# Head of a fused attention and gated-MLP kernel: another order for the V projections of the first chunk, and one load moved to SyncE's queue

## The chip, the cores and the metric

The kernel runs on one core of a Trainium2 chip. The metric is device time in microseconds (us) of one execution, the median over several runs.

The engines are named as in the profile: PE is TensorE's matmul, PEld its weight load, DVE is VectorE, ACT is ScalarE, POOL is GpSimd and SP is SyncE. SP does no arithmetic here: it issues DMA transfers. ACT can issue them too. Each engine works through its own instructions in order.

## The reference, cut to what matters

The input `x` has 2048 rows of 640 numbers in bf16. Its rows are normalised, and the result goes into two branches that are added to `x`.

```
def _A_ref(x, wqkv, wo):
    B, S, D = x.shape
    H = 32; Dh = D // H; W = 256
    qkv = (lambda x, *d: x.transpose(*d))((x @ wqkv).reshape(B, S, 3, H, Dh), 2, 0, 3, 1, 4)
    q, k, v = qkv[0], qkv[1], qkv[2]
    scores = jnp.einsum("bhqd,bhkd->bhqk", q, k) * (Dh ** -0.5)
    idx = jnp.arange(S)
    mask = (idx[:, None] - idx[None, :] >= 0) & (idx[:, None] - idx[None, :] < W)
    scores = jnp.where(mask[None, None], scores, -1e9)
    p = _softmax(scores, axis=-1)
    o = jnp.einsum("bhqk,bhkd->bhqd", p, v)
    return (lambda x, *d: x.transpose(*d))(o, 0, 2, 1, 3).reshape(B, S, D) @ wo

def _B_ref(x, w_gate, w_up, w_down):
    g = jnp.einsum("bsd,df->bsf", x, w_gate)
    u = jnp.einsum("bsd,df->bsf", x, w_up)
    h = _sigmoid(g) * u
    return jnp.einsum("bsf,fd->bsd", h, w_down)

x = A_x
xn = _layernorm(x, axis=-1)
return x + _A_ref(xn, A_wqkv, A_wo) + _B_ref(xn, B_w_gate, B_w_up, B_w_down)
```

The change touches the layer norm of the first 512 rows and their V columns, `xn @ wqkv[:, 1280:1920]`.

## The kernel before

**Chunks and blocks.** The 2048 rows are worked through in four chunks of 512 rows, and each chunk has four blocks of 128 rows, numbered 0 to 3. A block lies in SBUF with its 128 rows on the partitions. The later chunks' projections, the MLP matmuls and the attention steps are mixed by a small planner (`Fill`, L533) that hands out matmul work by cost between attention steps. The first chunk has nothing to be mixed with: its head is written out by hand at L614 to L648, one call after another, and the order of the calls is the order of the instructions on each engine (`tc.manual_schedule()`).

**What the head does for each block s of chunk 0.**

1. `load_rows(s, queue)` (L171) loads 128 x 640 numbers of `x` (160 KB).
2. Mean and deviation come in one of two ways. Blocks 0 and 2 use DVE: `ln_half` (L245) takes the statistics of one half of the columns, `ln_mv` (L251) joins the two halves, and `root` (L587) takes the square root on ACT. Blocks 1 and 3 use ACT: `mean_act` (L596) sums the row, `root_act` (L602) sums the squares and takes the root.
3. `norm` (L592) or `norm_act` (L608) takes the reciprocal and scales the rows, both on DVE.
4. `transpose_rows` (L272) turns the block on PE, five matmuls of 128 x 128 into a PSUM tile `pt`, and the function given as `copy` brings it into `xnT[0]`, on DVE or ACT. For block 0 this is done in two pieces.
5. `project_v(0, s, hf)` (L319) multiplies the block with one half of V's columns, `hf` 0 or 1, 320 each: a group of five matmuls into a PSUM tile. `copy_v` (L327) brings it to SBUF in bf16, on DVE or ACT, into `vt`. `proj_v` is the two together.

The group of block s and half hf is called "s, hf" or just the two digits, so 01 is block 0, second half. There are eight of them, and their PSUM tiles rotate through four buffers of `ps_d` (two warm-up tiles have used that pool before).

**The loads.** `load_v(hf)` (L174) loads one half of V's columns (400 KB), `load_wqkv(0)` and `load_wqkv(1)` the Q and the K columns (800 KB each), and `load_gu(0)` (L195) the first halves of the MLP's gate and up weights (960 KB each). All of these are issued by SP, one after the other, as are the rows of blocks 0, 1 and 3. The rows of block 2 are issued by ACT (L235), behind a first activation that loads ACT's table. Two `clear` transfers end the list; what SP issues next are the projected Q columns.

**After the head.** `g_qk(0)` (L360) projects Q and K of chunk 0, ten groups of five matmuls at L295. Each group's result is copied (DVE for Q, ACT for K), written to a scratch tensor in DRAM and read back, spread over the partitions as the scores need it (L311). Then `load_rest` (L203) issues the second halves of the MLP's weights, and the planner's mixture begins: gate and up matmuls (L401, L408), score steps (L472) with exponentials on ACT (L477) and masks on POOL (L480), the products with V (L504), and the output projections (L422, L429).

While ten matmuls on zeros (L236 to L239) run at the start, no rows have landed yet.

The head as it stands, with the eight groups:

```
transpose 0, 00, transpose 1, 01, 10, transpose 2, 11, 20, transpose 3, 21, 30, 31
```

Of the kernel before, what the change touches and what calls it, by code (L numbers as in the profile page):

```python
# [107 lines left out]
def kernel(  # L108
# [11 lines left out]
    nc = tc.nc  # L120
# [44 lines left out]
    def load_wqkv(part):  # L165
        nc.sync.dma_start(out=wqkv[:, :, part * D:(part + 1) * D],
                          in_=wqkv_r[:, :, part * D:(part + 1) * D])
# [3 lines left out]
    def load_rows(s, queue):  # L171
        queue.dma_start(out=xc[0][:, s, :], in_=xr[:, s, :])

    def load_v(hf):  # L174
        a = 2 * D + hf * HALF
        nc.sync.dma_start(out=wqkv[:, :, a:a + HALF], in_=wqkv_r[:, :, a:a + HALF])
# [2 lines left out]
    load_rows(1, nc.sync)  # L179
    load_v(0)  # L180
    load_rows(3, nc.sync)
    load_v(1)
    load_wqkv(0)
    load_wqkv(1)
# [47 lines left out]
    nc.gpsimd.memset(eps, EPS)  # L232
    scr = const.tile([P, 1], FP32, name="scr")
    nc.scalar.activation(out=scr, in_=eps, func=SQRT)
    load_rows(2, nc.scalar)  # L235
    for n in (6, 4):  # L236
        ps = ps_d.tile([P, CW], FP32, name="pwarm", tag="d")
        for k in range(n):
# [6 lines left out]
    def ln_half(c, s, a, stats=None):  # L245
        if a == 0:
            stats = lnp.tile([P, 2, nc.vector.BN_STATS_DIM], FP32, name="stats")
        nc.vector.bn_stats(out=stats[:, a, :], in_=xc[c][:, s, a * HALF:(a + 1) * HALF])  # L248
        return stats

    def ln_mv(stats, mv=None):  # L251
        if mv is None:
            mv = lnp.tile([P, nc.vector.BN_AGGR_DIM], FP32, name="mv")
        nc.vector.bn_aggr(out=mv, in_=stats)
        return mv

    def ln_block(c, s, mv=None):
        return ln_mv(ln_half(c, s, 1, ln_half(c, s, 0)), mv)
# [13 lines left out]
    def transpose_rows(s, copy, lo=0, hi=DC):  # L272
        pt = ps_h.tile([P, DC, P], BF16, name="pt")
        for d in range(lo, hi):
            nc.tensor.transpose(pt[:, d, :], xns[0, s][:, d * P:(d + 1) * P], ident)  # L275
        copy(out=xnT[0][:, lo:hi, s * P:(s + 1) * P], in_=pt[:, lo:hi, :])  # L276
# [42 lines left out]
    def project_v(c, s, hf):  # L319
        ps = ps_d.tile([P, CW], FP32, name="pv", tag="d")  # L320
        for d in range(DC):
            nc.tensor.matmul(ps[:, 0:HALF], lhsT=xnT[c][:, d, s * P:(s + 1) * P],  # L322
                             rhs=wqkv[:, d, 2 * D + hf * HALF:2 * D + (hf + 1) * HALF],
                             start=(d == 0), stop=(d == DC - 1))
        return ps

    def copy_v(c, s, hf, ps, copy):  # L327
        v3 = vt[c * SBC + s][:, 0:H * VW].rearrange("p (h d) -> p h d", d=VW)
        copy(out=v3[:, hf * 16:(hf + 1) * 16, 0:DH],  # L329
             in_=ps[:, 0:HALF].rearrange("p (h d) -> p h d", d=DH))  # L330

    def proj_v(c, s, hf, copy=nc.vector.tensor_copy):
        copy_v(c, s, hf, project_v(c, s, hf), copy)
# [253 lines left out]
    def root(mv):  # L587
        r = lnp.tile([P, 1], FP32, name="rstd")
        nc.scalar.activation(out=r, in_=mv[:, 1:2], func=SQRT, bias=eps)
        return r  # L590

    def norm(s, mv, r):  # L592
        nc.vector.reciprocal(r, r)
        norm_block(0, s, mv, r)

    def mean_act(s):  # L596
        xn = lnp.tile([P, D], BF16, name="xn")
        neg = lnp.tile([P, 1], FP32, name="neg")
        nc.scalar.activation(out=xn, in_=xc[0][:, s, :], func=IDENTITY, scale=-1.0 / D, accum_out=neg)
        return xn, neg  # L600

    def root_act(s, xn, neg):  # L602
        r = lnp.tile([P, 1], FP32, name="rstd")
        nc.scalar.activation(out=xn, in_=xc[0][:, s, :], func=SQUARE, bias=neg, accum_out=r)
        nc.scalar.activation(out=r, in_=r, func=SQRT, bias=eps, scale=1.0 / D)
        return r

    def norm_act(s, xn, neg, r):  # L608
        nc.vector.reciprocal(r, r)
        nc.vector.tensor_scalar(out=xn, in0=xc[0][:, s, :], scalar1=neg[:, 0:1],  # L610
                                scalar2=r[:, 0:1], op0=ADD, op1=MULT)
        xns[0, s] = xn
# [4 lines left out]
    act, dve = nc.scalar.copy, nc.vector.tensor_copy  # L617
# [7 lines left out]
    v00 = project_v(0, 0, 0)  # L625
    norm_act(1, xn1, neg1, r1)
    xn3, neg3 = mean_act(3)
    transpose_rows(1, act)
    mv2 = ln_block(0, 2)
    r2 = root(mv2)  # L630
    v01 = project_v(0, 0, 1)
    copy_v(0, 0, 0, v00, dve)
    norm(2, mv2, r2)
    r3 = root_act(3, xn3, neg3)
    v10 = project_v(0, 1, 0)
    copy_v(0, 0, 1, v01, dve)
    transpose_rows(2, dve)
    v11 = project_v(0, 1, 1)
    norm_act(3, xn3, neg3, r3)
    copy_v(0, 1, 0, v10, act)  # L640
    copy_v(0, 1, 1, v11, act)
    v20 = project_v(0, 2, 0)
    transpose_rows(3, dve)
    copy_v(0, 2, 0, v20, act)
    proj_v(0, 2, 1, dve)
    proj_v(0, 3, 0, act)
    proj_v(0, 3, 1, dve)
    nc.scalar.activation(out=scr, in_=neghalf[:, 0:1], func=EXP)  # L648
    banks.close()
    ps_s = banks.enter_context(tc.tile_pool(name="ps_s", bufs=1, space=bass.MemoryType.PSUM))  # L650
# [134 lines left out]
```

## Time and profile before

| what | value |
|---|---|
| runs | 314.15, 314.97, 314.70, 315.43 us; median 314.83 |
| the profiled execution | 314.15 us, its span 312.4 us |
| PE busy | 304.7 us, 98% of the span |
| PEld / DVE / ACT / POOL busy | 56% / 51% / 62% / 50% |
| granted TensorE clock in the record | 1.00 |
| moved by DMA | 35.71 MB, mean 114 GB/s |

The span runs from the first to the last instruction of the profiled execution; 1.75 us of its time lie around the span. A timeline line gives start, length, engine, line, operation, output and input, count, and in brackets how long the engine was idle before and what released it. Lengths of matmuls that follow each other overlap, since the array is pipelined: the step from one to the next is shorter than the length of one. The same holds to a smaller degree on DVE and ACT.

How the DMA engines stand in the head can be seen in the windows of 3 us: their busy share is 1.00 to 1.06 from 3 to 18 us and the rate 286 to 396 GB/s, so that transfers queue behind each other there; it falls to 0.43 between 27 and 30 us and is back at 1.00 or more from 33 us.

### The profile page before, as it was taken

What the parts mean: (1) busy time and instruction counts of PE and PEld (TensorE: products, weight loads), DVE (VectorE), ACT (ScalarE), POOL (GpSimd) and SP (SyncE); (2) the same over time, 40 slices, a digit from 0 to 9 for tenths busy, and PEclk for the clock granted to TensorE, in tenths of its full rate; (3) what the DMA queues carried; (4) which work ended last, traced back from release to release, by engine and by line L of the source; (5) the groups of instructions that cost most, each with busy time, mean ns of one, the idle gap of its engine ahead of it and who ended that gap; (6) DMA issues with size and microseconds to landing.
All of it is one profiled execution on the core that took longest, in us unless ns stands there. A gap on an engine that the chain in (4) does not pass through costs nothing.

```text
span 312.4 us, 10513 instructions
## 1 busy us (share of the span) xinstructions
PE 304.7 (98%) x4627; PEld 175.5 (56%) x4663; DVE 160.3 (51%) x316; ACT 192.2 (62%) x177; POOL 155.7 (50%) x239
## 2 busy tenths in 40 slices
PE   8999999999999999999999999999999999999995
PEld 3554444556557655644567665744556675544774
DVE  3643746548695264289826154362723536262523
ACT  5614787697764648787673647768585547778000
POOL 3000576576872827567382627546362835555000
PEclk9999999999999999999999999999999999999999
DMA  7995999664663153720025213630000213000002
GB/s 228 375 330 176 308 386 162 228 175 154 198 79 106 44 157 100 233 82 2 2 44 86 87 57 97 215 119 2 2 3 2 72 58 109 0 4 0 4 21 65
DMA packets 37614, 35.71 MB, mean 114 GB/s; under 512 B 10272, under 2 KB 37024, under 8 KB 37536
## 3 DMA queue, kind: packets, MB, share of 16 engines
q1 hardware_dynamic: 37136, 34.76, 38.3%
q8 instruction: 36, 0.59, 0.8%
q10 hardware_dynamic: 432, 0.28, 0.3%
q14 instruction: 10, 0.08, 0.1%
HBM read 23.63 MB, written 10.26 MB: 108 GB/s over the span
## 4 chain that ended last, share of the span: by engine, by line
PE 95%; DMA 2%; DVE 1%; issue 1%; DVEq 0%
PE y L422 17%; PE pu L408 17%; PE pg L401 17%; PE pqk L295 14%; PE ps L472 9%; PE y L429 7%; PE acc L504 7%; PE pv L322 7%; DMA xc<-in_A_x_dram 2%; DVE stats L248 0%; PE pt L275 0%; DVE h L412 0%; DVE xn L268 0%; DVE v L329 0%; DVE xn L433 0%
## 5 line engine op out<-in xcount | busy, mean ns | idle before, releaser
L480 POOL TENSOR_SCALAR_AFFINE_SELECT pT<-pT 128x512 bf16<-128x512 bf16 (+2 forms) x192 | 147.2, 798 | 129.1 <-ACT pT L477 129.0
L477 ACT ACTIVATE pT<-ps 128x2048 bf16<-128x2048 f32 x76 | 142.7, 1878 | 63.7 <-PE ps L472 59.0
L412 DVE SCALAR_TENSOR_TENSOR h<-th,pu 128x512 bf16<-128x512 f32 x48 | 32.7, 682 | 60.8 <-PE pu L408 49.6
L408 PE MATMUL pu<-xnT,wu 128*128 128x512 bf16 x228 | 59.2, 380 | 0.7
L401 PE MATMUL pg<-xnT,wg 128*128 128x512 bf16 x225 | 57.8, 380 | 1.0 <-issue 0.5
L422 PE MATMUL y<-wd,h 128*128 128x320 bf16 (+2 forms) x396 | 57.0, 296 | 0.0
L295 PE MATMUL pqk<-xnT,wqkv 128*128 128x512 bf16 x191 | 45.5, 381 | 0.5
L422 PEld LDWEIGHTS <-h 128*128 128x128 bf16 x396 | 36.5, 98 | 14.3
L404 ACT ACTIVATE th<-pg 128x512 f32<-128x512 f32 x48 | 28.6, 596 | 14.5 <-PE pg L401 13.9
L401 PEld LDWEIGHTS <-wg 128*128 128x128 bf16 x240 | 22.3, 98 | 25.3 <-issue 0.2
L408 PEld LDWEIGHTS <-wu 128*128 128x128 bf16 x240 | 21.9, 98 | 25.4 <-issue 0.6
L472 PEld LDWEIGHTS <-kT 20*64 20x64 bf16 x1856 | 20.6, 103 | 24.2 <-issue 22.3
L295 PEld LDWEIGHTS <-wqkv 128*128 128x128 bf16 x200 | 22.6, 119 | 18.0 <-issue 0.6
L472 PE MATMUL ps<-qT,kT 20*64 20x128 bf16 (+4 forms) x1856 | 32.5, 239 | 0.0
L433 DVE SCALAR_TENSOR_TENSOR rows<-y,rows 128x320 bf16<-128x320 f32 x30 | 14.5, 489 | 33.2 <-PE y L429 33.0
L514 DVE STREAM_TRANSPOSE t<-acc 128x512 f32<-128x512 f32 x32 | 22.0, 710 | 18.1 <-PE acc L504 17.8
L526 DVE TENSOR_TENSOR on<-t,rec 128x320 bf16<-128x320 f32 (+4 forms) x48 | 27.5, 574 | 1.1
L322 PE MATMUL pv<-wqkv,xnT 128*128 128x320 bf16 x160 | 24.1, 302 | 0.3 <-DVE xnT L276 0.2
L429 PE MATMUL y<-wo,oc 128*128 128x320 bf16 (+2 forms) x165 | 24.2, 295 | 0.0
L504 PE MATMUL acc<-pT,v 128*32 128x64 bf16 (+3 forms) x1376 | 23.2, 223 | 0.1
L504 PEld LDWEIGHTS <-v 128*32 128x32 bf16 x1376 | 18.6, 97 | 7.9 <-ACT pT L477 1.7
L322 PEld LDWEIGHTS <-xnT 128*128 128x128 bf16 x160 | 14.9, 98 | 7.3 <-DVE xnT L276 1.0
(46 smaller groups left out, 134.3 us busy)
## 6 DMA issues: line engine op xcount, KB each, us to landing
qT<-sq SPq DMA_DIRECT2D x7, 512.0 KB, 5.5
sq<-st SPq DMA_DIRECT2D x20, 128.0 KB, 4.0
sk<-st SPq DMA_DIRECT2D x20, 128.0 KB, 2.8
rows<-in_A_x_dram SPq DMA_DIRECT2D x15, 160.0 KB, 2.2
out_dram<-rows SPq DMA_DIRECT2D x15, 160.0 KB, 1.8
kT<-sk SPq DMA_DIRECT2D x4, 512.0 KB, 5.7
wg<-in_B_w_gate_dram SPq DMA_DIRECT2D x2, 960.0 KB
wu<-in_B_w_up_dram SPq DMA_DIRECT2D x2, 960.0 KB, 9.9
```

Source lines behind the costliest of these rows:

```text
L295: nc.tensor.matmul(ps, lhsT=wt[:, m, :], rhs=xnT[c][:, d, :], start=(d == 0), stop=(d == DC - 1))
L322: nc.tensor.matmul(ps[:, 0:HALF], lhsT=xnT[c][:, d, s * P:(s + 1) * P], rhs=wqkv[:, d, 2 * D + hf * HALF:2 * D + (hf + 1) * HALF], start=( ...
L401: nc.tensor.matmul(pg, lhsT=part(wg, d, f), rhs=xnT[c][:, d, :], start=(d == 0), stop=(d == DC - 1))
L404: nc.scalar.activation(out=th, in_=pg, func=TANH, scale=0.5)
L408: nc.tensor.matmul(pu, lhsT=part(wu, d, f), rhs=xnT[c][:, d, :], start=(d == 0), stop=(d == DC - 1))
L412: nc.vector.scalar_tensor_tensor(out=h, in0=th, scalar=1.0, in1=pu, op0=ADD, op1=MULT)
L422: nc.tensor.matmul(y[:, 0:cut[1] - cut[0]], lhsT=ht[c, f][:, s * P:(s + 1) * P], rhs=wd[:, f, cut[0]:cut[1]], start=(f == 0), stop=False)
L429: nc.tensor.matmul(y[:, 0:cut[1] - cut[0]], lhsT=oc[c, m][:, s * P:(s + 1) * P], rhs=wo[:, m, cut[0]:cut[1]], start=False, stop=(m == DC - 1))
L472: nc.tensor.matmul(ps[hf * U:(hf + 1) * U, i, col * U:(col + n) * U], lhsT=qk["k", kc, g // GH][32 * i:32 * i + DH, g % GH, key:key + U], ...
L477: nc.scalar.activation(out=pt[:, :, 0:CW], in_=ps, func=EXP, scale=SCALE)
L480: nc.gpsimd.affine_select(out=out, in_=in_, pattern=[[0, HG], [0, n], [sign, width]], compare_op=GE, fill=0.0, base=base, channel_multipli ...
L504: nc.tensor.matmul(acc[32 * i:32 * i + 32, q * U:(q + n) * U], lhsT=v[:, h * VW:h * VW + 32], rhs=pt[:, i, col * U:(col + n) * U], start=( ...
```

## The change

The rows of block 2 are issued by SP, between those of block 3 and V's second half, and no longer by ACT. Then the hand-written order of the head is another one:

- TensorE's order becomes transpose 0, 00, transpose 1, 10, 01, transpose 3, 11, transpose 2, 30, 31, 20, 21. The number of matmuls is the same.
- The copy of transpose 1 goes from ACT to DVE, and stands on DVE between the two halves of block 2's statistics.
- ACT's square sum and root for block 3 come ahead of the root for block 2, and DVE scales block 3 ahead of block 2.
- The copies of 00 and 01 go from DVE to ACT. ACT now copies 00, 10, 01, 11, 30 and 20; DVE copies 31 and 21.

DMA transfers signal their landing through eight counters that are used in turn, and a transfer waits until the one that used its counter before has landed. With block 2's rows at another place in the list, the transfers of the head wait for other ones than before.

```
@@ -179,6 +179,7 @@
     load_rows(1, nc.sync)
     load_v(0)
     load_rows(3, nc.sync)
+    load_rows(2, nc.sync)
     load_v(1)
     load_wqkv(0)
     load_wqkv(1)
@@ -232,7 +233,6 @@
     nc.gpsimd.memset(eps, EPS)
     scr = const.tile([P, 1], FP32, name="scr")
     nc.scalar.activation(out=scr, in_=eps, func=SQRT)
-    load_rows(2, nc.scalar)
     for n in (6, 4):
         ps = ps_d.tile([P, CW], FP32, name="pwarm", tag="d")
         for k in range(n):
@@ -625,26 +625,26 @@
     v00 = project_v(0, 0, 0)
     norm_act(1, xn1, neg1, r1)
     xn3, neg3 = mean_act(3)
-    transpose_rows(1, act)
-    mv2 = ln_block(0, 2)
+    r3 = root_act(3, xn3, neg3)
+    half2 = ln_half(0, 2, 0)
+    transpose_rows(1, dve)
+    mv2 = ln_mv(ln_half(0, 2, 1, half2))
+    v10 = project_v(0, 1, 0)
+    copy_v(0, 0, 0, v00, act)
     r2 = root(mv2)
     v01 = project_v(0, 0, 1)
-    copy_v(0, 0, 0, v00, dve)
+    norm_act(3, xn3, neg3, r3)
     norm(2, mv2, r2)
-    r3 = root_act(3, xn3, neg3)
-    v10 = project_v(0, 1, 0)
-    copy_v(0, 0, 1, v01, dve)
+    copy_v(0, 1, 0, v10, act)
+    transpose_rows(3, dve)
+    v11 = project_v(0, 1, 1)
+    copy_v(0, 0, 1, v01, act)
     transpose_rows(2, dve)
-    v11 = project_v(0, 1, 1)
-    norm_act(3, xn3, neg3, r3)
-    copy_v(0, 1, 0, v10, act)
     copy_v(0, 1, 1, v11, act)
-    v20 = project_v(0, 2, 0)
-    transpose_rows(3, dve)
-    copy_v(0, 2, 0, v20, act)
-    proj_v(0, 2, 1, dve)
     proj_v(0, 3, 0, act)
     proj_v(0, 3, 1, dve)
+    proj_v(0, 2, 0, act)
+    proj_v(0, 2, 1, dve)
     nc.scalar.activation(out=scr, in_=neghalf[:, 0:1], func=EXP)
```

## The prediction

> **What bounds the kernel now.** I read the page's chain of waits first, then the same chain for the first 15 us, then the timelines of TensorE, its weight loads, VectorE and ScalarE there, and last the stretch after 30 us where weights land late. The chain's shares by engine:
>
> ```profile
> PE 95%; DMA 2%; DVE 1%; issue 1%; DVEq 0%
> ```
>
> TensorE sets the end everywhere but in the head. So a change in the head is worth what it takes from the time at which TensorE is through with V and begins the Q/K projections (pqk). The head's part of the chain (start, length, what):
>
> ```profile
> 0.80 2.34 DMA xc<-in_A_x_dram
> 3.17 4.63 DMA xc<-in_A_x_dram
> ...
> 7.82 0.90 DVE stats L248 x2
> ...
> 9.51 0.46 DVE xn L268
> ...
> 10.01 0.45 PE pt L275 x5
> ```
>
> The second load is row block 2, issued on ScalarE's queue at 3.17 and landed at 7.80. Its statistics, root and scaling follow, and TensorE gets block 2's transpose only at 10.01. TensorE and its weight loads in that time:
>
> ```profile
> 5.50 0.74 PE L275 MATMUL pt<-ident,xn 128*128 128x128 bf16 x5
> 6.47 1.12 PE L322 MATMUL pv<-wqkv,xnT 128*128 128x320 bf16 x5 [0.24 <-DVE xnT L276]
> 7.43 0.44 PE L275 MATMUL pt<-ident,xn 128*128 128x128 bf16 x5
> 7.92 1.59 PE L322 MATMUL pv<-wqkv,xnT 128*128 128x320 bf16 x10
> 10.01 0.45 PE L275 MATMUL pt<-ident,xn 128*128 128x128 bf16 x5 [0.50 <-DVE xn L268]
> ...
> 12.02 2.28 PE L322 MATMUL pv<-wqkv,xnT 128*128 128x320 bf16 x15
> 14.13 0.38 PE L295 MATMUL pqk<-xnT,wqkv 128*128 128x512 bf16 x1
> ```
>
> Call T1 the transposes of block 1 and "10" the V group of block 1, first half. Fifteen matmuls stand between 12.02 and 14.13, less one wait of 0.07: 2.04/15 = 0.136 us each, 0.68 for a group. A transpose set holds TensorE 0.28 (10.01 to the next group at 10.30 on the full timeline; 11.74 to 12.02). From T1's last issue at 7.71 (7.43 + 0.28) to pqk at 14.13 are 6.42 us; seven groups and two sets are 7 x 0.68 + 2 x 0.28 = 5.32. TensorE waits 1.10 in it: 0.21 for group 01 (7.71 to 7.92), 0.68 for T2 (9.33 to 10.01), 0.2 in three small ones.
>
> **The change part by part.** Everything up to T1 is untouched, so T1's results stand at 7.87 (7.43 + 0.44).
>
> *T1's copy goes from ScalarE to VectorE, behind the first half of block 2's statistics.* The rows:
>
> ```profile
> 6.72 0.45 DVE L610 TENSOR_SCALAR xn<-xc,neg,rstd 128x640 bf16<-128x640 bf16 x1
> 7.82 0.89 DVE L248 BATCH_NORM_STATS2 stats<-xc 128x6 f32<-128x320 bf16 x2 [0.65 <-DMA xc<-in_A_x_dram]
> 10.50 0.49 DVE L276 COPY xnT<-pt 128x640 bf16<-128x640 bf16 x1
> ...
> 7.91 0.69 ACT L276 COPY xnT<-pt 128x640 bf16<-128x640 bf16 x1 [1.00 <-PE pt L275]
> ```
>
> VectorE is free at about 7.13 (its next operation starts 0.41 after a 0.45 one). The half statistics take 0.49: 7.13 to 7.62, if block 2 is there. The copy then waits only for T1 and starts at 7.91 as ScalarE's did, but takes 0.49 for 0.69: done at 8.40 for 8.60. A weight load follows a copy by 0.05 (10.99 to 11.04), so group 10 starts at 8.45.
>
> *Block 2's load moves to SyncE's queue.* Its landing there is not in the trace. Lower bound: block 3's rows (same size, issued at 2.19 directly ahead, awaited by ScalarE until 6.08) plus 164 kB at the 357 GB/s of the window from 6 to 9 us, 0.46: 6.5. Upper bound: V's second half, issued at 2.76 and first used at 7.92, took at most 5.16; from the new issue at 2.63 that is 7.8. I take 6.5, the row it is nearest to. The copy of T1 is hit only from a landing after 7.42 (7.91 - 0.49). At 7.8 it would start at 8.21 (statistics step 0.41), 0.30 later.
>
> The Trainium skill (DMA: Bandwidth & Descriptors, "Issuing engines are not separate DMA queues") says that all queues run on the same 16 engines and interleave, and another issuer saves only issue time. That speaks against a gain from the move. By it the load would come only its earlier issue sooner, at about 7.3; the trace's 4.63 us on ScalarE's queue against 3.9 on SyncE's speaks for a little more. By the rule as by the row, the copy of T1 is not delayed.
>
> SyncE issues one more load (0.43, the L176 row's length), so V's second half, the Q and K weights, the gate weights and the clears are issued 0.43 later. V's second half, in use at 7.92 before, is wanted at 9.14 now; the Q weights (issued at 3.24, 6.9 to landing: 10.1) at 13.8. SyncE stands idle from 10.7 to 16.1, where the delay ends. Without that cover group 01 would lose at most 0.43. ScalarE loses the issue (0.44 at 3.17); its next operation, at 3.65, waited for block 1's rows, and that chain has 0.7 to spare (root ready at 5.80, used at 6.53): nothing.
>
> *TensorE's new order: 10, 01, T3, 11, T2, 30, 31, 20, 21.* 10 is now first after T1 with nothing to cover the copy, so TensorE waits 7.71 to 8.45 = 0.74. Is each input there in time after that?
> - 01 at 9.14 needs block 0 and V's second half: there.
> - T3 at 9.82 needs block 3 scaled. VectorE: statistics' second half 8.32 to 8.80, aggregate 0.21, reciprocal 0.15, scaling 0.45, with gaps of 0.04: 9.68. ScalarE's root for it: mean 6.08 to 6.91, square 0.81, read and root to 8.2. Margin 0.14.
> - 11 at 10.10: there. T2 at 10.78 needs block 2 scaled: root 9.07 to 9.36, then reciprocal and scaling after block 3's: 10.3.
> - 30 at 11.06 needs T3's copy: T3's results at 10.3, VectorE free then, 0.49 and 0.05: 10.85.
> - 31, 20, 21 follow; T2's copy is done at 11.8, wanted at 12.42.
>
> So the wait is 0.74 for 1.10. pqk starts at 8.45 + 5.32 = 13.77 against 14.13: **0.36 earlier**.
>
> *Copies of V.* ScalarE gets 00 and 01 (2 x 0.43) and loses T1's (0.69): 0.17 more, under its 3.4 us of idle before 14.1. VectorE gets 0.49 and loses 0.98. The accumulators rotate over four buffers: 30 takes that of 00, freed at 8.6, wanted at 11.06; the others have more room. Without the cover the Exp table load at 14.10 would slip, and its first use is past 31 us. All this costs nothing.
>
> *Does 0.36 last?* The transfers after 24 us are paced by the DMA engines (share 1.00 and above from 33 to 42 us), so landings need not move with TensorE. The tight one is the second half of the up weights:
>
> ```profile
> 30.57 0.53 SPq L197 DMA_DIRECT2D wu<-in_B_w_up_dram  x1
> ...
> DMA to landing us min/median/max: 9.9/9.9/9.9
> ...
> 40.79 0.76 PEld L408 LDWEIGHTS <-wu 128*128 128x128 bf16 x5
> ```
>
> It lands at 40.47 and is used at 40.79: 0.32 of room, less 0.05 from landing to use. If the landing stays, 0.27 of the gain survives; if it moves along, 0.36. I take 0.3. After that, the chain is TensorE to the end.
>
> **The sum.** The profiled execution: 314.15 - 0.3 = 313.85. It is the lowest of four (to 315.43), 0.68 under their median of 314.83, so the forecast for a median is 314.5.
>
> The Trainium skill (TensorE: Matmul & The Clock Gate, Part 1) says that the array runs at half rate until a free-running window of about 3.4 us was busy. From the first warm-up matmul at 1.25 the rise could fall anywhere from 4.7 to 8.1, another place in each run, an estimate from that page. This trace has it inside group 00: T0 took 0.74 and T1 0.44. By an early rise the gain would be near 0.5, by the latest about -0.2, since the old order's wait for T2 hides cold matmuls and the new order has no such wait left. The sum goes by the trace.
>
> **The rivals.**
> - *Hidden anyway*, 314.8. The weights' landing at 40.47 slips by a little, or the transposed rows of the second chunk (by DMA, wanted near 56 us) do, and the 0.3 is gone. For it: 0.32 of room. Against it: those loads start from Q/K spreads that partly follow TensorE.
> - *All of the 1.10 goes*, 313.7. It needs T1's copy to be covered; in the new order nothing stands between T1 and group 10, so only runs that scatter low would show it.
> - *The clock rises later* (slower). Place: the 0.74 hole at 7.71, in the change's kernel alone. A cold group costs about 0.65 more (the ten warm-up matmuls of 512 columns took 4.45, about 0.43 each, where five later ones step in 1.08, 0.22 each; so 320 columns 0.27 for 0.136), T1 0.30 (0.74 - 0.44), the rest of group 00 about 0.4. If the rise waits until 10 and 01 are done: 0.4 + 0.30 + 2 x 0.65 = 2.0 less 0.36, 1.6 slower: 316.5. It decides from a rise after 7.7. Against it: the rise at about 7 lies ahead of the first changed instruction.
> - *The load isn't sooner on SyncE's queue.* At the bound of 7.8 the gain is 0.06: 314.8.
>
> **How the numbers follow.** Within 0.3% (0.94 us, about what a measurement of this kernel can tell from no change; the four runs spread over 1.28): the forecast 0.46, hidden 0.13, load not sooner 0.07: 0.66. Faster 0.18: all of the 1.10 gone 0.12, low scatter 0.06. Slower 0.16: the clock 0.11, high scatter 0.05. Predicted is the likeliest, 314.5. The range: down to the full 1.10, 313.7; up through no gain to the highest run before, 315.5; the clock's 316.5 is left out.
>
> **What would show it.** T1's copy on VectorE at 7.9 for 0.5 us, group 10 at about 8.45, no wait of TensorE over 0.1 from there to pqk, pqk at 13.8; block 2's statistics starting at 7.1 with no wait for the load; the weight load of L408 near 40.5. Wrong: block 2's load awaited past 7.4, T3 waiting for its scaling, cold matmuls (0.27 a step) in groups 10 or 01, or pqk at 13.8 with the end not moved.

## The result, and the profile after

The changed kernel took 313.77 us (median of 34 runs, 313.02 to 316.30); the kernel before took 315.01 us over 56 runs (314.08 to 315.99). The ratio is 0.9967, with a 95% interval of 0.9959 to 0.9975: 1.04 us, or 0.33%, faster (0.0033 x 315.01; by the two medians 1.24). A run more than 1.5% above the fastest of its kernel counts as slow and enters no ratio; that was one run, in call 3. The gain is just past the 0.3% that the prediction had named as its border, and about three times the 0.3 us that it had worked out.

The profiled execution of the changed kernel took 313.39 us with a span of 311.7, against 314.15 and 312.4. The shares by engine of the chain of waits, on the page:

```profile
PE 95%; DMA 1%; DVE 1%; issue 1%; SPq 1%; DVEq 0%
```

TensorE still sets the end, and DMA's share went from 2% to 1%. The head of that chain (start, length, what):

```profile
2.76 4.14 DMA xc<-in_A_x_dram
...
6.92 0.49 DVE stats L248
7.42 0.44 DVE xnT L276
...
7.91 1.53 PE pv L322 x10
```

Block 2's rows land at 6.90 instead of 7.80. But they are still in the chain: the first half of their statistics stands on VectorE ahead of T1's copy, and the copy ends at 7.86. They hold it up by next to nothing, though, since T1's own results stand only at 7.32 (6.87 + 0.45):

```profile
7.36 0.49 DVE L276 COPY xnT<-pt 128x640 bf16<-128x640 bf16 x1
```

From 7.91 TensorE waits no more than 0.07 in all up to the Q/K projections (13.30 - 7.91 = 5.39, where the prediction's sum has 5.32). TensorE's timeline in the same stretch:

```profile
5.33 0.45 PE L275 MATMUL pt<-ident,xn 128*128 128x128 bf16 x5
6.12 0.85 PE L322 MATMUL pv<-wqkv,xnT 128*128 128x320 bf16 x5 [0.34 <-DVE xnT L276]
6.87 0.45 PE L275 MATMUL pt<-ident,xn 128*128 128x128 bf16 x5
7.91 1.53 PE L322 MATMUL pv<-wqkv,xnT 128*128 128x320 bf16 x10 [0.59 <-DVE xnT L276]
...
13.30 2.54 PE L295 MATMUL pqk<-xnT,wqkv 128*128 128x512 bf16 x10
```

Two things are to be seen. Block 0's transposes take 0.45 here and took 0.74 before, so the clock rose earlier in this execution, ahead of anything that TensorE does in another order: the recorded clock goes to full at 4.88, against 7.06 in the first profile. T1 starts at 6.87 for 7.43 by it. And the Q/K projections (pqk) start at 13.30 for 14.13: 0.83 earlier, where the prediction had 0.36. The next line is from the weight loads near 40 us:

```profile
40.28 0.76 PEld L408 LDWEIGHTS <-wu 128*128 128x128 bf16 x5 [0.36 <-DMA wu<-in_B_w_up_dram]
```

The seventh up group started at 40.79 before, without a wait. Now TensorE's weight loads stand 0.36 until the second half of the up weights has landed, and start 0.51 ahead: 0.32 of the 0.83 is gone there. (The chain of this profile names VectorE's scaling, which ended at the same time; call 3 separates the two.) Score matmuls near 203 us that take 0.52 for 0.36 cost another 0.16. What is left when VectorE's last operation starts, before and after:

```profile
309.06 0.29 DVE xn L433
```
```profile
308.71 0.29 DVE xn L433
```

0.35 of the gain is left there, and 0.76 between the two whole executions. So 0.41, more than half, arises behind the last matmul, where little more than the last output transfers is under way. The table further below comes back to this.

### The profile page after: what moved, and what is told of

Same layout as the page of the kernel before. It is cut to its first block, busy times and chain, and to the rows that moved or that the text cites. A ratio compares the mean times of both kernels' runs of the same rounds, so it can differ in the third digit from the quotient of the medians.

```text
span 311.7 us, 10513 instructions
## 1 busy us (share of the span) xinstructions
PE 304.0 (98%) x4627; PEld 175.2 (56%) x4663; DVE 160.0 (51%) x315; ACT 192.1 (62%) x178; POOL 155.7 (50%) x239
## 4 chain that ended last, share of the span: by engine, by line
PE 95%; DMA 1%; DVE 1%; issue 1%; SPq 1%; DVEq 0%
PE y L422 17%; PE pu L408 17%; PE pg L401 16%; PE pqk L295 14%; PE ps L472 9%; PE y L429 7%; PE pv L322 7%; PE acc L504 7%; DMA xc<-in_A_x_dram 1%; DVE h L412 0%; SPq L172 0%; DVE xn L268 0%; PE pt L275 0%; DVE stats L248 0%; DVE xnT L276 0%
```

## The experiments

Twelve more measurements were made in three calls. The kernels of one call shared a chip and its runs of the kernel before, whose median was 315.66, 315.11 and 314.96 us in the three calls; so a kernel is compared with others of its own call.

### Call 1: which part does it, and how steady is the head?

**The kernel before once more**, without an edit.

> The kernel before, unchanged, for a second profile and for the spread of its head. Open is why the change gave about 1.0 us where the prediction's sum has 0.36 at the head and 0.3 at the end. Theory 'clock': the clock's rise moves from run to run, but the Q/K projections start near 14.1 as in the first profile, since the wait for block 2 hides it; the first profile is typical. Theory 'landing': block 2's rows land at another time in each run on ScalarE's queue, mostly later than the first profile's 7.80, and the projections start later than 14.3 here. Times the same as before within 0.1% by both.

Measured: 315.28 us (12 runs), ratio 0.9992 (0.9976 to 1.0008): no difference. Its median is 0.38 below that of the other runs of the same kernel in the call, which shows how little a difference of that size between two medians says. The chain in its profile:

```profile
3.19 4.85 DMA xc<-in_A_x_dram
...
10.26 0.45 PE pt L275 x5
```

Block 2's rows land at 8.04, 0.24 later than in the first profile. T2 starts 0.25 later, and pqk at 14.38, also 0.25 later. In these two profiles the landing moves and takes pqk with it one for one.

**The load alone.**

```
     load_rows(3, nc.sync)
+    load_rows(2, nc.sync)
     load_v(1)
...
-    load_rows(2, nc.scalar)
```

> The old order with block 2's rows on SyncE's queue, between block 3's and V's second half. Theory 'load' (the gain comes from block 2's rows being there sooner): rows at 6.9, statistics from 7.1, block 2 scaled at about 9.5 for 9.95, its transposes at 9.6 for 10.01, Q/K projections at about 13.7; most of the gain, a ratio of 0.997 to 0.998. Theory 'order' (the gain comes from the new order and the faster copy of T1): less than a third of the gain, 0.999 to 1.000, with the projections at 13.9 or later, since V's second half, issued later, now holds back group 01.

Measured: 313.98 us (11 runs), ratio 0.9952 (0.9935 to 0.9969). By the runs the load alone brings the gain here. The head of its profiled execution, 314.57 us, is not what the first theory expected: the loads were late in it (V's first half landed at 6.45, against 5.57 in the first profile; block 2's rows at 7.35), and pqk started at 14.13, no earlier than in the first profile. V's second half, now behind block 2's rows, landed at 8.62 and held back group 01, as the second theory has it. Where the gain of the runs arises is therefore not shown by this profile alone.

**The order alone.**

```
     nc.scalar.activation(out=scr, in_=eps, func=SQRT)
+    load_rows(2, nc.scalar)
...
-    load_rows(2, nc.sync)
```

applied to the changed kernel, so that only the new order is left.

> The new order with block 2's rows left on ScalarE's queue. Theory 'load': the statistics' first half waits for the rows until 7.8 and the copy of T1 stands behind it, so T1's copy starts at 8.2 and group 10 at 8.75, projections at 14.0 to 14.1; ratio 0.999 to 1.000, and slower in executions in which the rows land later than 7.9. Theory 'order': group 10 by 8.5, projections by 13.8, ratio 0.997 to 0.998.

Measured: 315.59 us (12 runs, 314.40 to 318.14), ratio 1.0009 (0.9985 to 1.0034). The order alone brings no gain that shows. The chain:

```profile
3.19 5.54 DMA xc<-in_A_x_dram
...
8.76 0.49 DVE stats L248
9.25 0.40 DVE xnT L276
...
9.70 1.53 PE pv L322 x10
```

The rows land at 8.73, and the copy of T1 waits behind their statistics. Group 10 starts at 9.70 and pqk at 15.02. By the prediction's own sum a landing after 7.86 makes the new order slower than the first profile's 14.13. The profiled execution, 316.53 us, was 0.94 above the median of its runs, and the head is not all of it: near 58 us TensorE waited another 1.05 for the second chunk's transposed rows.

**The changed kernel, with the late weights in pieces.** The second halves of the gate and up weights are loaded in two column pieces each.

```
-    def load_gu(k):
-        for t, w in ((wg, B_w_gate), (wu, B_w_up)):
-            nc.sync.dma_start(out=t[k], in_=w.rearrange("(c p) f -> p c f", p=P)[:, :, k * FS:(k + 1) * FS])
+    def load_gu(k, parts=1):
+        n = FS // parts
+        for lo in range(0, FS, n):
+            for t, w in ((wg, B_w_gate), (wu, B_w_up)):
+                nc.sync.dma_start(out=t[k][:, :, lo:lo + n],
+                                  in_=w.rearrange("(c p) f -> p c f", p=P)[:, :, k * FS + lo:k * FS + lo + n])
...
-            load_gu(k)
+            load_gu(k, 2)
```

> The changed kernel with the second-half gate and up weights loaded in two pieces each (columns 0 to 383 of both, then the rest), so that the first up columns land near 37.5 rather than 40.2. In the profile of the changed kernel TensorE came 0.84 ahead to 39.9 and started the seventh up group at 40.28, 0.51 ahead of the kernel before. Theory 'landing cap': that group then starts as early as TensorE comes, and the end is 0.2 to 0.4 us earlier than the changed kernel, a ratio to the kernel before of 0.9955 to 0.9965. Theory 'no cap' (the wait there was VectorE's scaling, as the chain has it, or a later wait takes the gain anyway): the same as the changed kernel, 0.9967 within 0.0006.

Measured: 313.48 us (6 runs), ratio 0.9943 (0.9922 to 0.9964). The interval is too wide to tell it from the changed kernel, which was not in this call; call 3 puts them side by side. In its profile pqk starts 0.45 ahead of the first profile, and the seventh up group, at 40.33 without a wait, 0.46: nothing is lost near 40 us.

### Call 2: load against order on one chip, and what makes the load late

**The changed kernel** and **the load alone**, both again.

> The changed kernel, unchanged, on the same chip as the next three. Theory 'load' (in the first call the old order with the load on SyncE's queue gave 0.9952, the new order with the old load 1.0009): 0.995 to 0.997, and equal to the load alone within 0.001. Theory 'both' (the new order adds the 0.36 that the prediction worked out): 0.001 faster than the load alone. In its profile: block 2's rows between 6.6 and 7.4, Q/K projections at 13.2 with an early rise of the clock and at 13.5 to 13.8 with one near 7.

> The old order with block 2's rows on SyncE's queue, beside the changed kernel on one chip. Theory 'load': 0.995 to 0.997, equal to the changed kernel within 0.001; Q/K projections at 13.6 to 14.0. Theory 'both': 0.001 slower than the changed kernel.

Measured: 313.92 us (12 runs), ratio 0.9960 (0.9940 to 0.9979), for the changed kernel; 314.41 us (12 runs), 0.9978 (0.9956 to 1.0001), for the load alone. By the medians the order adds 0.49 us to the load, but the intervals overlap, and the second one includes no change; in call 1 the load alone had been 1.68 below the kernel before, here 0.70. So the times leave open what the order adds. The chain of the load alone tells where it would come from:

```profile
3.23 5.91 DMA wqkv<-in_A_wqkv_dram
...
9.18 1.52 PE pv L322 x10
```

In the old order group 01 is next after T1. With block 2's rows moved ahead of it, V's second half lands at 9.14 in this execution and becomes the wait; pqk starts at 14.65. In the changed kernel group 10 comes first, needs only V's first half, and group 01 finds V's second half there. An estimate, from the landings and transposes of the two profiles of the load alone: in the new order their pqk would have started 0.36 and 0.28 earlier.

**The load on ScalarE's queue, but first of all.**

```
     load_rows(1, nc.sync)
+    load_rows(2, nc.scalar)
...
-    load_rows(2, nc.scalar)
```

applied to the kernel before; the load is now ScalarE's first instruction, issued at 0.79.

> The old order with block 2's rows still on ScalarE's queue, but as its first instruction, ahead of the activation table, so issued at about 0.8 rather than 3.17. Theory 'place in the line' (what counts is when the load is issued, not by which engine): rows by 4.5, block 0's and block 1's up to 0.5 later since they share the DMA engines; no wait for block 2 before its transposes beyond that for ScalarE's root, projections at 13.7 to 14.0, ratio 0.996 to 0.999. Theory 'queue' (ScalarE's queue is served behind SyncE's backlog): rows after 7 as before, projections at 14.1 to 15.0, ratio 1.000.

Measured: 314.35 us (12 runs), ratio 0.9983 (0.9962 to 1.0003), pqk at 14.05. Block 2's rows landed at 4.05, between blocks 0 (3.87) and 1 (4.44). Nothing waits for them any more; the chain goes another way:

```profile
2.76 5.54 DMA wqkv<-in_A_wqkv_dram
...
8.34 1.57 PE pv L322 x10
```

V's second half takes the place of the wait again, and blocks 0 and 1 came 0.7 to 0.8 later, where 0.5 was expected. pqk is just past the expected 13.7 to 14.0. ScalarE's queue as such isn't slow.

**The changed kernel with the load one place later**, behind V's second half.

```
-    load_rows(2, nc.sync)
     load_v(1)
+    load_rows(2, nc.sync)
```

> The changed kernel with block 2's rows on SyncE's queue behind V's second half rather than ahead of it. Theory 'load': the rows land at 7.9 to 8.6, the statistics' first half and behind it the copy of T1 wait for them, one for one, so group 10 starts 0.41 + 0.49 + 0.05 after the landing, near 9.1 (8.4 with the rows at 7), and the projections at 14.2 to 14.8; ratio 0.999 to 1.001. Theory 'order': 0.996 to 0.998, projections by 13.8.

Measured: 314.40 us (12 runs), ratio 0.9981 (0.9959 to 1.0003), 0.48 above the changed kernel by median. The chain:

```profile
3.23 4.64 DMA xc<-in_A_x_dram
...
7.89 0.49 DVE stats L248
8.38 0.40 DVE xnT L276
...
8.83 1.53 PE pv L322 x10
```

On SyncE's queue, issued at 3.23, the rows land at 7.86. On ScalarE's queue, issued at 3.17, they had landed at 7.80. So the earlier landing comes not from the queue but from the place: ahead of the 400 KB of V's second half. Group 10 starts 0.97 after the landing, by the 0.41 + 0.49 + 0.05 of the expectation (0.95), and pqk at 14.15, as in the first profile of the kernel before. The median lies 0.71 below the kernel before's all the same, though the ratio's interval reaches 1.0003.

### Call 3: the cap near 40 us, and an attempt to go further

**The changed kernel a third time, and with the weights in pieces.**

> The changed kernel, unchanged, as the mark for the next three on the same chip: 0.995 to 0.997 of the kernel before.

> The changed kernel with the second-half gate and up weights in two pieces each, now beside the changed kernel. Theory 'landing cap' (part of the head's gain is lost near 40 us, where the seventh up group waits for weights that land at 40.2 to 41.1): 0.2 to 0.5 us faster than the changed kernel by median. Theory 'no cap', or the transposed rows of the second chunk, wanted near 56 us, take the gain instead: equal within 0.15 us.

Measured: 314.10 us (12 runs), ratio 0.9975 (0.9962 to 0.9989), and 313.63 us (6 runs), 0.9955 (0.9938 to 0.9973). The pieces are 0.47 faster by median; the intervals overlap. In both profiles pqk starts at 13.39, so the two heads end alike. The changed kernel's TensorE at 31 us and its chain at 41 us read:

```profile
31.24 0.42 PE L472 MATMUL ps<-qT,kT 20*64 20x320 bf16 x16 [0.38 <-DMA kT<-sk]
```
```profile
31.45 9.60 DMA wu<-in_B_w_up_dram
41.04 0.05 issue
41.09 1.25 PE pu L408 x5
```

Of the 0.74 that the head was ahead of the first profile of the kernel before, 0.48 is lost at 31.24 (31.50 there), where K columns are read back late. Then the up weights, issued at 31.45 instead of 30.57, land at 41.04 after another 0.58 of waiting, and TensorE comes out 0.29 behind. With the pieces, the weight loads and the later chain:

```profile
40.05 0.76 PEld L411 LDWEIGHTS <-wu 128*128 128x128 bf16 x5
```
```profile
51.08 4.53 DMA xnT<-xn
55.61 0.04 issue
55.65 2.32 PE pqk L298 x10
```

Here the whole 0.74 passes 40 us, and 0.44 of it passes the next late landing, the second chunk's transposed rows at 55.61 (pqk of that chunk at 55.65, for 56.09 in the first profile). The profiles show the wait for the up weights, which is gone in both profiles with the pieces, and the wait behind it. VectorE's scaling was not the cause: with the pieces it ends at 40.34, and the group starts ahead of that, at 40.05. That the wait for the up weights is worth the 0.47 of the medians is likely, not shown: 6 runs stand against 12, and part of the difference between these two profiles arose at 31 us.

**All rows ahead of V.** The row loads of blocks 3 and 2 go ahead of V's first half, block 2's statistics ahead of block 0's copy, group 00 behind T1, group 01 behind transpose 3, and ScalarE's root for block 2 ahead of its copy of 00; the second kernel has the weights in pieces too.

```
     load_rows(1, nc.sync)
-    load_v(0)
     load_rows(3, nc.sync)
     load_rows(2, nc.sync)
+    load_v(0)
     load_v(1)
...
     norm(0, mv0, r0)
+    half2 = ln_half(0, 2, 0)
...
-    v00 = project_v(0, 0, 0)
...
-    half2 = ln_half(0, 2, 0)
+    half2 = ln_half(0, 2, 1, half2)
     transpose_rows(1, dve)
-    mv2 = ln_mv(ln_half(0, 2, 1, half2))
+    v00 = project_v(0, 0, 0)
+    mv2 = ln_mv(half2)
     v10 = project_v(0, 1, 0)
+    r2 = root(mv2)
     copy_v(0, 0, 0, v00, act)
-    r2 = root(mv2)
-    v01 = project_v(0, 0, 1)
...
     transpose_rows(3, dve)
+    v01 = project_v(0, 0, 1)
     v11 = project_v(0, 1, 1)
```

> The changed kernel with the rows of all four blocks ahead of V's first half, statistics of block 2 ahead of block 0's copy, and group 00 behind T1. Theory 'straggler' (the landing of everything behind V's first half hangs on the slowest of sixteen shares of that load, 5.4 to 7.1 in the profiles so far, and block 2's rows stand behind it in the changed kernel too): rows by 4.8 in every execution, T1's copy no longer behind a late statistics, group 00 at 7.2 or where V's first half lands (6.5 to 8), Q/K projections at 13.2 to 13.6, 0.2 to 0.5 us faster than the changed kernel and with less spread. Theory 'all loads are slow together': rows of block 2 land after 5.5 in slow executions, the projections at 13.8 or later, no gain.

> The last two edits together. If the cap near 40 us and the head are in series: the fastest of the four, 0.5 to 0.9 us under the changed kernel, ratio to the kernel before 0.993 to 0.994. If the gain of the head is lost at the next late landing (transposed rows near 56 us): as the better of the two alone.

Measured: 314.58 us (12 runs, up to 318.16; 314.30 over the eleven that enter the ratio), ratio 0.9983 (0.9967 to 0.9999), and 313.84 us (12 runs), 0.9966 (0.9948 to 0.9984). Both misses: no gain over the changed kernel, and none over the pieces alone. The chain of the first:

```profile
2.65 5.25 DMA wqkv<-in_A_wqkv_dram
...
7.94 1.52 PE pv L322 x10
```

V's first half now lands at 7.90, and group 00 waits for it; pqk starts at 13.93, and at 13.58 with the pieces. Block 2's rows were there by 5.64, not by the expected 4.8: in this execution one of the sixteen shares of the row loads was late too. The idea that only V's load has late shares falls.

### The profiled heads together

Landings are the last of the sixteen shares in the trace's record, times in us. "T1 through" is the end of T1 on TensorE; "tail" runs from the end of the last matmul to the end of the span; the last column is the profiled execution's own time.

| kernel | V's first half landed | block 2 landed | T1 through | pqk starts | 7th up group | tail | time |
|---|---|---|---|---|---|---|---|
| before | 5.57 | 7.80 | 7.87 | 14.13 | 40.79 | 3.40 | 314.15 |
| before again | 5.80 | 8.04 | 7.92 | 14.38 | 41.04 | 3.54 | 314.53 |
| order alone | 6.38 | 8.73 | 7.55 | 15.02 | 41.68 | 3.36 | 316.53 |
| ScalarE's queue, first | 6.71 | 4.05 | 8.26 | 14.05 | 40.70 | 3.66 | 314.33 |
| load alone | 6.45 | 7.35 | 7.79 | 14.13 | 41.16, waits | 3.21 | 314.57 |
| load alone again | 7.10 | 8.01 | 8.26 | 14.65 | 41.31 | 2.97 | 315.01 |
| changed | 6.01 | 6.90 | 7.32 | 13.30 | 40.28, waits | 3.00 | 313.39 |
| changed again | 6.61 | 7.50 | 7.77 | 13.93 | 41.13, waits | 3.12 | 314.56 |
| changed, third | 6.11 | 7.00 | 7.42 | 13.39 | 41.08, waits | 3.08 | 314.10 |
| one place later | 5.91 | 7.86 | 7.34 | 14.15 | 40.81 | 3.22 | 314.01 |
| pieces | 5.73 | 6.61 | 7.76 | 13.68 | 40.33 | 2.84 | 313.18 |
| pieces again | 5.70 | 6.57 | 7.43 | 13.39 | 40.05 | 2.84 | 313.13 |

Read five things from it.

- In the kernel before, pqk starts 6.33 and 6.34 after block 2's landing. In the new order T1's copy waits for two things, and the later one decides. Group 10 starts either 0.97 after the landing (9.70 with the order alone, 8.47 in "changed again", 8.83 one place later) or 0.59 to 0.60 after T1 is through (7.91 in "changed", 8.02 in "changed, third", 8.35 and 8.02 with the pieces). "Changed, third" and "pieces again" have landings 0.43 apart, T1 at the same time, and pqk at 13.39 both.
- T1 depends on the clock. It was through by 7.43 where the recorded clock rose between 4.8 and 5.4 and V's first half was there by 6.1, and at 7.76 with the pieces, where the clock rose at 6.84.
- On ScalarE's queue behind V's second half, block 2 lands 2.23 to 2.35 after V's first half, on SyncE's in its new place 0.87 to 0.91 after it: about 1.35 sooner for the same pace of the DMA engines.
- That pace differs from run to run by up to 1.5 us at V's first half; the first profile of the kernel before is the earliest of all in that column.
- The tail is 3.36 to 3.66 in the four profiles in which ScalarE issues block 2's rows, and 2.97 to 3.22 in the six listed in which SyncE does, whatever the order; with the pieces it is 2.84. So some 0.4 us of the change's gain seems to come with the load's queue and to have nothing to do with the head. What makes the difference is open. The trace records 8 KB transfers of the instruction queue there, beside the last output; the last of them starts 1.3 to 1.7 after the last matmul in the first group, 0.9 to 1.2 in the second, and ahead of the last matmul with the pieces. That these hold up the last output is likely; no run tested it.

## Why the prediction was right or wrong

The time of 313.77 lies within the range, 313.7 to 315.5, close to its lower end, and the direction was forecast. The likeliest case, a change within 0.3% and a time of 314.5, was too cautious: the measured gain is 1.04 us where it had 0.3.

- **"pqk starts at 8.45 + 5.32 = 13.77 against 14.13: 0.36 earlier"** is the step that was mis-sized; the pair of profiles has 0.83. The rule behind it was right: T1's results, then the copy, then 5.32 of matmuls. Where the clock rose late again and the rows were there early (the first profile with the pieces), pqk started at 13.68, near the 13.77. The inputs were those of one execution. First, "T1's results stand at 7.87": in the changed profile they stood at 7.32, since the clock rose earlier, so that group 10 came at 7.91 for 8.45. That is 0.54, and small waits behind it take 0.07 back. The prediction had an early rise beside its sum, with a gain near 0.5. Second, the 14.13 of the kernel before holds for rows that land at 7.80, and both profiles of that kernel have V's first half earlier than all three of the changed kernel. An estimate: at the 6.01 and 6.61 of the changed kernel's profiles, the old order with its old load would start pqk at about 14.6 and 15.2 (2.23 and 6.33 more).
- **The median.** The first profile's time was the lowest of the four runs, 0.68 under their median, and the prediction carried that gap over to the forecast as a constant. It may well hold the very wait that the change shortens; no trace of a run near the median shows it.
- **"After that, the chain is TensorE to the end"** put nothing behind the last matmul. Between the two profiles 0.41 arises there. The 0.3 that was worked out for the end agrees with the 0.35 at the last VectorE operation, but by luck in part: the head gave 0.47 more than its sum, and more was lost on the way.
- **Block 2's landing.** The lower end of 6.5 was taken; with the new place of the load 6.90, 7.50 and 7.00 were measured, and 6.61 and 6.57 with the pieces. "The copy of T1 is hit only from a landing after 7.42" held for T1 as in the first profile. With T1 through at 7.32 the border is near 6.9, so that the landing of 6.90 was just level with it; in "changed again" the landing of 7.50 decided. TensorE's 0.74 of waiting was about right in length (0.76, from 7.15 to 7.91 in the changed profile).
- **The copy on VectorE, the order of the inputs and the copies of V** went as worked out: 0.49 for the copy, and in the changed profile from group 10 on no wait of TensorE over 0.1 us. But the order's worth was put wrongly. Alone it brings nothing that shows (1.0009). Beside the load it takes V's second half off TensorE's path, by the estimate of call 2 some 0.3 us at the head. That this second half would have been the next wait without the new order, the prediction did not see; it had at most 0.43 for it.
- **"0.27 of the gain survives"** near 40 us was right in mechanism, place and kind: the changed kernel waits there in all three profiles, for 0.36 to 0.59, and by the medians 0.47 more comes through with the pieces. In size it mattered more, since more gain arrived there. The rival's second landing, near 56 us, is the next cap, as the profile with the pieces shows. The prediction let the landing stay or move with TensorE; it moved from run to run instead, between 40.24 and 41.09 in the three profiles.
- **The clock as the slower case** did not come. The rise lay between 4.72 and 7.15 in the 13 profiles that record it, always ahead of group 10, and in the first pair of profiles an early one made the gain larger. The Trainium skill (TensorE: Matmul & The Clock Gate, Part 1) has the window free-running and the rise at another place in each run; the profiles agree, with block 0's transposes at 0.74 in some and 0.44 in others. The same part gives the variation as 500 ns either way; the 2.4 us measured here are more.
- **The load's queue.** The Trainium skill (DMA: Bandwidth & Descriptors, "Issuing engines are not separate DMA queues") says that transfers of all issuing engines run on the same 16 DMA engines and interleave, and that another issuer saves only issue time. The runs agree that the queue does not decide: issued at 3.23 by SyncE or at 3.17 by ScalarE, block 2 landed at 7.86 and 7.80. What the prediction drew from it, that the load would come only its earlier issue sooner, at about 7.3, missed what the sum's own 6.5 had: an issue 0.41 earlier, at 2.76, put the load ahead of 400 KB.

That one pair of profiles shows 0.76 and the runs 1.04 would fit the table, if the typical execution has later landings than the first profile. How the landings of the runs without a profile were spread was not recorded, so this last part is argued and not shown, and so is how the 1.04 divides between the head and the tail.

## What to carry to other kernels

A profile is one execution. Where its time lies under the median of the runs, ask which waits in it vary, and whether the change frees the path of one of them: here the old order always waited for one load, and the new one for the later of a load and of matmuls that depend on the clock. While the DMA engines were behind, a load's place in the line decided its landing, not the queue that issued it; the place ahead of V's second half was worth 1.1 us on one queue (block 2 landed 0.89 and 1.95 after V's first half) and about 1.35 with the change of queue. Then follow a gain in the head to the next landings that don't move with it: here there were two, in one execution a third, and loading the late weights in two pieces each let more of the gain through by the medians (313.63 for 314.10 us, on one chip). And compare the two profiles at the last instruction as well as at the end of the span.

## What the runs showed of the hardware

One share in sixteen can be far behind. V's first half, 400 KB in sixteen shares, had fifteen landed by 5.40 and the last at 7.10 in one execution, and by 5.49 and 5.57 in the first profile. The loads that stand behind it have a late share too, and their last shares keep their distance: on SyncE's queue block 2's rows landed 0.9 after it each time. The same was seen in row loads that stood ahead of any load of V (fifteen by 4.25, the last at 5.17). What makes that share late is open; it was not tried.
